# Windowed attention and a squared-ReLU MLP in one kernel: batches three to seven as one run of key tiles, with a refitted DMA model in the planner

## The chip, the cores and the metric

The kernel runs on one core of one Trainium2 chip. The metric is the device time of one execution in microseconds; lower is better. The engines are TensorE (PE; PEld is its weight load), VectorE (DVE), ScalarE (ACT), GpSimd (POOL) and SyncE (SP), each with its own queue of instructions that it works off in order. SP and ACT also issue DMAs.

## What is computed

The inputs q, k and v are float32 of 8 batches x 8 heads x 576 positions x 64. Attention is local: a position sees those at most 32 away. Its result, as 4608 tokens of 512, goes through an MLP.

```python
scores = q @ k.T / sqrt(64)                  # per batch and head
scores = where(abs(i - j) <= 32, scores, -1e9)
x = softmax(scores) @ v                      # -> (4608, 512), token = batch*576 + position
h = maximum(x @ w_in, 0.0)                   # 512 -> 2048
out = (s * h * h + b) @ w_out                # 2048 -> 512
```

## The kernel before

**Attention by units.** Keys are cut in tiles of 64. A unit is two neighbouring key tiles of one batch, stacked on the 128 partitions; a batch has 9 tiles, so five units, the fifth with a single tile (`NTILE = 9`, `NUNIT = 5`, `tiles`, L589). For each key tile, `qk_part` (L592) multiplies the 64 keys with a window of 128 queries, from 32 before the tile to 32 after it, for all 8 heads: 16 small matmuls into the PSUM tensor SC for a full unit. `exp_mask` (L606) takes the exponential on ACT (L620) and multiplies it by a band mask on VectorE (L624), which zeroes what is further than 32 away. `av_part` (L632) then multiplies with V (L650); each 64-query piece sums up to two key tiles, one of them perhaps in the unit before. V has a 65th column of ones, so that the same matmul gives the softmax sum. `finish` (L662) takes the reciprocal (L670), normalizes into XN (L672), and transposes the 128 or 96 finished tokens into XT: on TensorE and ACT for batches 0 to 2 (L679, L684; `XPE = 3`), with DMA transposes issued by SP from batch 3 on (L690). XT is a ring of 2048 token columns. One TensorE task of a unit joins the AV of the unit before and the scores of its own (`pe_part`, L695; `LAG = 1`), and the scores are put between the two halves of the AV.

**Loads.** Batches 0 and 1 come through SP (L493, L478) and are transposed on TensorE (L505). From batch 2 on ACT issues the loads (`LATE = 2`): q and k in three pieces per batch (`piece`, L523: 512 rows of q, 512 of k, the last 64 of both), V in one load per unit (`load_v`, L474, five staging slots VST). Each q/k piece is cast to bf16 in two halves (L543), on the engines that `CASTE` names: both on GpSimd for batch 2, both on VectorE for the batches after. SP then transposes it by DMA (L550), q straight into QT, k into KTR, from where GpSimd copies it in order into KT (L560), four or five copies per batch. QT and KT have two slots, used in turn by the batches. V is cast into VB (L485), two tensors of five slots.

**The MLP.** Tokens are worked in blocks of 96, 128, 288 and then eight of 512. `s1` (L838) computes 16 tiles of h^T (L849), ReLU on ACT (L856) and the square on VectorE (L858); `s2` (L862) multiplies with w_out (L867), L880 adds what s and b give, and SP stores the result (L884).

**Who sets the order.** Nothing here is in order by the program text. `add` (L75) makes a task with its engine, an estimated cost, what it reads and writes, a key and a slack. `plan` (L106) plays the whole kernel through with these costs: it takes, again and again, the task that can start first (ties by key), and so fixes each engine's queue. DMAs are in the play too: a load has a number of rows and a price per row (`dma=("l", 16, 92.0)`), the rings of SP and ACT share the bandwidth (`serve`, L119), a task that reads a loaded buffer is planned to start `slack` ns after the load's planned end at the earliest (`release`, L155), and an issue from ACT waits until its ring has at most `CALM` rows left (`space`, L139). The keys are due times: `due` (L403) asks when the MLP block that holds a unit's first token begins. `emit` (L212) writes the queues with the semaphores that the dependences need: on the chip the order is fixed, and an engine whose next task isn't ready stands still. The loads up to batch 1 have keys below -100 and are chained in a fixed order on SP.

The lines of `plan` that set when the engine is free again after it issues a DMA:

```python
            full = max(st, space(t.stream, self.RING))
            if t.dma[0] == "t":
                free[t.stream] = full + t.cost
            else:
                free[t.stream] = max(st + t.cost, full)
```

Of the kernel before, what the change touches and what calls it, by code (L numbers as in the profile page):

```python
# [10 lines left out]
S = 576  # L11
# [7 lines left out]
NUNIT = (NTILE + 1) // 2  # L19
VW = 66  # L20
# [9 lines left out]
XPE = 3  # L30
PACE = ((-1, -1, -1),) * 3
CASTS = 20.0
LATE = 2
AFTERV = 4
KTV = 0
CASTE = (("pool", "pool"), ("dve", "dve"))
SLACK = (1000.0, 2000.0, 3000.0, 3000.0)
# [23 lines left out]
class _Graph:  # L61
# [6 lines left out]
    RING, CALM, ISSUE, WRITE = 112.0, 40.0, 1400.0, 600.0  # L68
# [37 lines left out]
    def plan(self):  # L106
# [63 lines left out]
        while len(order) < len(self.tasks):  # L170
            best = None
            for s in self.STREAMS:
                for t in open_[s]:
                    at = max(free[s], t.ready)
                    if s == "act" and t.dma is not None:
                        at = max(at, space(s, self.CALM))
                    c = (at, t.key, t.n)
                    if best is None or c < best[0]:
                        best = (c, t)
            st = best[0][0] if best else 1e9  # L180
            done, clock[0] = serve(rings, clock[0], max(st, clock[0]))
            room.clear()
            if done is not None:
                done.fin = clock[0] + self.WRITE
                release(done)
                continue
            assert best is not None, "a cycle"
            t = best[1]
            open_[t.stream].remove(t)
            t.start = st  # L190
            free[t.stream] = t.fin = st + t.cost
            order.append(t)
            for u in t.next:
                u.left -= 1
                if u.left == 0:
                    open_[u.stream].append(u)
            if t.dma is None:
                release(t)
                continue
# [4 lines that stand above are left out]
                free[t.stream] = max(st + t.cost, full)  # L204
            rings[t.stream].append([t, (full if t.dma[0] == "t" else st) + self.ISSUE, float(t.dma[1])])
            room.clear()
        self.order = order
# [96 lines left out]
def bass_sliding_window_symmetric__then__act_starrelu_kernel(  # L304
# [22 lines left out]
    with ExitStack() as es:  # L327
# [24 lines left out]
        VB = [sb((128, NUNIT, H, VW), BF16, "vb") for _ in range(2)]  # L352
        EXS = sb((128, NEX, 2, NPAIR, 128), BF16, "ex")
        EX = [EXS[:, i, :, :, :] for i in range(NEX)]
        MASK = sb((128, 128), BF16, "mask")
# [43 lines left out]
        def unit_rows(m):  # L399
            lo = max(0, 128 * m - WIN)  # L400
            return lo, min(S, 128 * m + 128 - WIN)

        def due(b, m):  # L403
            tok = b * S + unit_rows(m)[0]
            blk = next(x for x in range(NM) if TBLK[x][0] + TBLK[x][1] > tok)
            f = (tok - TBLK[blk][0]) / TBLK[blk][1]
            before = PH[blk] - PH[blk - 1] if blk > 0 else 4.0
            return PH[blk] - 14.0 - (1.0 - f) * before
# [20 lines left out]
        for p0 in (0, 64):  # L429
            band(MASK[p0:p0 + 64, :], ONESW[p0:p0 + 64, :], ("MASK", p0), 0, 64, -96)  # L430
        for i in range(2):
            for c0 in (0, WIN + S):
                zero("dve", QT[i][:, :, c0:c0 + WIN], ("QTZ", i, c0), 150, key=-98 if i == 0 else -20)
            add("dve", lambda e, i=i: e.memset(VB[i].rearrange("p t h c -> p (t h) c")[:, :, D:D + 1], 1.0), 150,
                writes=[("VBO", i)], key=-57 if i == 0 else -20)
# [12 lines left out]
        def load_weights(which, i, x, key, eng):  # L448
# [6 lines left out]
            else:  # L455
# [4 lines left out]
                dma=("l", 16, 92.0) if which == "in" else ("l", 32, 50.0))  # L460
# [5 lines left out]
        def paced(b, u):  # L466

            return land["av", b - 1, u] if u >= 0 else land["av", b - 2, NUNIT + u]

# [4 lines left out]
        def load_v(b, t, key, waits=()):  # L474

            n = min(128, S - 128 * t)
            add(late(b),
                lambda e: e.dma_start(VST[0:n, t, :, :], v[b, :, 128 * t:128 * t + n, :].rearrange("h p d -> p h d")),  # L478
                650.0, writes=[("VST", t)], key=key, dma=("l", n // 2, 23.0), waits=waits)
            land["v", b, t] = g.tasks[-1]  # L480

        def cast_v(b, t, key, eng, slack):
            slot, n = b % 2, min(128, S - 128 * t)
            add(eng, (lambda e: e.copy(VB[slot][0:n, t, :, 0:D], VST[0:n, t, :, :])) if eng == "act" else
                (lambda e: e.tensor_copy(VB[slot][0:n, t, :, 0:D], VST[0:n, t, :, :])),  # L485
                {"act": 617.0, "dve": 420.0, "pool": 750.0}[eng],
                reads=[("VST", t)], writes=[("V", slot, t)], key=key, slack=slack)

        def load_pair(b, name, pr, key, load_key, banks, eng, slack):
# [6 lines left out]
                600.0, writes=[("STG", si)], key=load_key, dma=("l", 8, 112.0))  # L496
# [26 lines left out]
        def piece(b, parts, key, waits):  # L523
# [16 lines left out]
                dma=("l", sum(n for _, _, n, _ in parts) // 8, 68.0))  # L540
# [26 lines left out]
        def later(b, key):  # L567
# [6 lines left out]
            for i, parts in enumerate(((("q", 0, 512, 0),), (("k", 0, 512, 0),), (("q", 512, 64, 0), ("k", 512, 64, 32)))):  # L574
                piece(b, parts, key + 0.01 * i, [paced(b, PACE[min(b, 4) - 2][i])] +
                      ([land["v", b - 1, AFTERV]] if b > (1 if LATE == 2 else 2) and AFTERV >= 0 else []))
# [8 lines left out]
        def buffers(b, u):  # L585
            n = b * NUNIT + u
            return EX[n % NEX], n % NEX, EX[(n - 1) % NEX], (n - 1) % NEX

        def tiles(u):  # L589
            return [j for j in (2 * u, 2 * u + 1) if j < NTILE]  # L590

        def qk_part(b, u, hps=(0, 1)):  # L592
            slot = b % 2
            fns = [lambda e, pr=pr, j=j, hp=hp: e.matmul(  # L594
                SC[64 * (j % 2):64 * (j % 2) + 64, hp, pr * 128:pr * 128 + 128],
                lhsT=KT[slot][64 * hp:64 * hp + 64, pr, 64 * j:64 * j + 64],
                rhs=q_window(b, pr, j)[64 * hp:64 * hp + 64], start=True, stop=True)
                for pr in range(NPAIR) for j in tiles(u) for hp in hps]
            lo, hi = max(0, 128 * u - WIN), min(S, 128 * u + 128 + WIN)
            reads = [("QT", slot, x, pr) for x in pieces(lo, hi, 64) for pr in range(NPAIR)]  # L600
            reads += [("KT", slot, x, pr) for x in tiles(u) for pr in range(NPAIR)]
            if u == 0:
                reads.append(("QTZ", slot, 0))
            if u == NUNIT - 1:
                reads.append(("QTZ", slot, WIN + S))
            return fns, reads, [("SC", hp) for hp in hps], 230.0 if len(hps) == 2 or u == NUNIT - 1 else 440.0  # L606

        def exp_mask(b, u, hps=((0, 1),)):
            key = due(b, u)
            ex, ei, _, _ = buffers(b, u)  # L610
            n = 64 * len(tiles(u))
            for hs in hps:
                dst, src = ex[0:n, hs[0]:hs[-1] + 1, :, :], SC[0:n, hs[0]:hs[-1] + 1, :].rearrange("p i (a c) -> p i a c", a=NPAIR)
                flat = dst.rearrange("p i a c -> p (i a) c")
                if b > 1:
                    flat_src = src.rearrange("p i a c -> p (i a) c").rearrange("p a (i c) -> p a c i", i=4)
                    flat_dst = flat.rearrange("p a (c i) -> p a c i", i=4)
                else:
# [4 lines left out]
                mask = MASK[0:n, :].rearrange("p (one c) -> p one c", one=1).to_broadcast((n, 4 * len(hs), 128))  # L623
                add("dve", lambda e, flat=flat, mask=mask: e.tensor_tensor(flat, flat, mask, ALU.mult),  # L624
                    130 + 0.53 * 512 * len(hs), reads=[("E", ei, hp, pr) for hp in hs for pr in range(NPAIR)] + [("MASK", p0) for p0 in (0, 64)],
# [6 lines left out]
        def av_part(b, u):  # L632


            slot = b % 2
            ex, ei, px, pi = buffers(b, u)
            bank, res = av_banks(b, u)
# [3 lines left out]
            def put(h, x, g):  # L641
# [3 lines left out]
                if not 0 <= j < NTILE:  # L645
                    return []
# [6 lines left out]
                    rhs=VB[slot][64 * g:64 * g + 64, j // 2, h, 0:D + 1], start=first, stop=True,  # L653
# [4 lines left out]
            reads = [("E", x, hp, pr) for x in ({ei, pi} if u > 0 else {ei}) for hp in (0, 1) for pr in range(NPAIR)]  # L658
            reads += [("V", slot, x) for x in ({u, u - 1} if u > 0 else {u})] + [("VBO", slot)]
            return fns, reads, res, 340.0  # L660

        def finish(b, u, key=None):  # L662
            key = due(b, u) if key is None else key
            n = b * NUNIT + u
            bank, avr = av_banks(b, u)
            av = bank.rearrange("p i (a c) -> p (i a) c", a=4)
            r0, r1 = unit_rows(u)
# [9 lines left out]
            if b < XPE:  # L677
# [8 lines left out]
            else:  # L686
                cuts = {x0, x0 + r1 - r0} | {x for x in range(XR, B * S, XR) if x0 < x < x0 + r1 - r0}
                cuts = sorted(cuts | ({x0 + WIN} if u == 0 else set()))
# [42 lines left out]
        def first_exp(dst, src, np_, sc, res, key):  # L731
# [5 lines left out]
                130 + 0.53 * 256 * n, reads=res + [("MASK", p0) for p0 in (0, 64)], writes=res, key=key)  # L737
# [8 lines left out]
        def unit(b, u):  # L746

            ripe = last[0] if len(last) >= LAG else None
            t = pe_part(due(*(ripe or (b, u))), av_part(*ripe) if ripe else None, qk_part(b, u))
# [5 lines left out]
        def close(t=None):  # L755
# [3 lines left out]
            closed[0] = bu[0] * S + unit_rows(bu[1])[1]  # L759
# [3 lines left out]
        def attention():  # L763
# [27 lines left out]
            for t in ORDER0:  # L791
                if t < 8:
                    load_v(0, t, nxt())
# [9 lines left out]
            for t in range(NUNIT):  # L803
                load_v(1, t, nxt())
# [8 lines left out]
            for b in range(2, B):  # L813
                later(b, due(b, 0) - 24.0)
                for t in range(NUNIT):
                    load_v(b, t, due(b, t) - 35.0, waits=[paced(b, PACEV[min(b, 4) - 2][t])] + ([land["kt", 2, 0]] if b == 2 and KTV else []))
                    cast_v(b, t, due(b, t) - 4.0, EV2[t], SLACK[3])
                for u in range(NUNIT):
                    unit(b, u)
                    yield closed[0]  # L820
            while last:
                close()
# [170 lines left out]
```

The softmax here doesn't subtract the row's maximum and nothing guards it: scores larger than these inputs give would overflow.

## Time and profile before

| | |
|---|---|
| median of 6 runs | 326.03 us (323.84 to 328.3) |
| the profiled execution | 327.07 us |
| its span, first to last instruction | 325.3 us |
| TensorE busy | 297.9 us (92%) |
| VectorE busy | 205.4 us (63%) |
| ScalarE busy | 141.0 us (43%) |
| GpSimd busy | 66.8 us (21%) |
| DMA | 56.70 MB, mean 174 GB/s |
| w_in matmuls L849, w_out matmuls L867 | 140.9 us, 139.6 us busy |
| exponentials L620 | 35 of 1023 ns mean |
| mask multiplies L624 | 35 of 742 ns mean |
| q/k casts L543 | 30 of 676 ns mean on VectorE, 6 on GpSimd |
| K copies L560 | 30 of 1072 ns mean on GpSimd |
| DMA transposes into XT, L690 | 32 |

The span is what the trace covers; the execution's own time is 1.8 us longer. A row of waits has the engine and line that waited, what released it, the time in all, how often, and the longest. A row of a timeline has start, duration, engine and line, operation, tiles (out<-in) and how many neighbouring instructions are merged in it; brackets hold the idle time before. "SPq" and "ACTq" are issues of DMAs from these engines' queues: their duration is how long the queue was held.

### The profile page before, as it was taken

The numbers are of one execution on the slowest core, as the hardware profiler recorded it, in microseconds if no ns is written. First come the engines' busy times: TensorE is split into PE (matmuls) and PEld (weight loads), VectorE is DVE, ScalarE is ACT, GpSimd is POOL, SyncE is SP. The second block draws the span as 40 slices with busy tenths as digits, with TensorE's granted clock in tenths as the row PEclk, the third lists the DMA queues.
The fourth block names the chain that finished last, engine by engine and source line by source line (L and its number), as shares of the span: only waits on it lengthen the run. The fifth ranks groups of instructions, "written<-read, shape, count | busy, mean of one in ns | idle before, by whom it ended". The sixth has DMA issues, their size and how long they took to land.

```text
span 325.3 us, 8084 instructions
## 1 busy us (share of the span) xinstructions
PE 297.9 (92%) x3410; PEld 162.6 (50%) x3452; DVE 205.4 (63%) x402; ACT 141.0 (43%) x219; POOL 66.8 (21%) x78
## 2 busy tenths in 40 slices
PE   3687898999998997989999999999999999999995
PEld 2575676755554443444444444444444444444442
DVE  2752588876878894679767868786865443332411
ACT  3645366445523772445225553553454433333200
POOL 3346455464106000420060006000600000000000
PEclk9999999999999999999999999999999999999999
DMA  7999999897896999899948995999612111000021
GB/s 235 280 241 348 360 229 335 279 206 212 202 229 185 268 123 128 177 302 134 249 124 251 166 222 116 195 222 218 154 57 67 50 46 62 34 32 32 34 94 68
DMA packets 104580, 56.70 MB, mean 174 GB/s; under 512 B 77216, under 2 KB 96160, under 8 KB 104544
## 3 DMA queue, kind: packets, MB, share of 16 engines
q1 hardware_dynamic: 62208, 34.94, 44.1%
q10 hardware_dynamic: 42336, 21.24, 31.0%
q8 instruction: 27, 0.44, 0.6%
q14 instruction: 9, 0.07, 0.1%
HBM read 36.70 MB, written 9.44 MB: 142 GB/s over the span
## 4 chain that ended last, share of the span: by engine, by line
PE 73%; DMA 15%; DVE 6%; issue 3%; POOL 1%; ACT 1%; SPq 0%; POOLq 0%
PE o L867 33%; PE w L849 31%; DMA stg<-in_moe_w_in_dram 5%; PE avn L650 4%; DMA stg<-in_moe_w_out_dram 3%; DMA vst<-in_v_dram 3%; DMA xt<-xn 3%; PE sc L594 2%; DVE ex L624 1%; PE o L890 1%; DVE gt L858 1%; DVE xn L672 1%; DVE vb L485 1%; PE sc L505 1%; DMA stg<-in_q_dram 1%
## 5 line engine op out<-in xcount | busy, mean ns | idle before, releaser
L849 PE MATMUL w<-xt,win 128*128 128x512 bf16 (+3 forms) x679 | 140.9, 344 | 6.3 <-issue 2.4
L867 PE MATMUL o<-wout,gt 128*128 128x512 bf16 (+1 forms) x623 | 139.6, 357 | 4.9 <-DVE wout L462 2.4
L856 ACT ACTIVATE r<-w 128x512 bf16<-128x512 f32 (+2 forms) x152 | 86.7, 575 | 115.8 <-PE w L849 99.9
L858 DVE TENSOR_TENSOR gt<-r 128x512 bf16<-128x512 bf16 (+2 forms) x152 | 72.8, 484 | 72.1 <-ACT r L856 71.2
L867 PEld LDWEIGHTS o<-wout,gt 128*128 128x128 bf16 x640 | 60.9, 98 | 64.4 <-DVE wout L462 2.7
L849 PEld LDWEIGHTS w<-xt,win 128*128 128x128 bf16 x704 | 61.9, 101 | 60.0 <-ACT r L856 2.4
L560 POOL COPY kt<-ktr 128x512 bf16<-128x512 bf16 (+1 forms) x30 | 32.2, 1072 | 131.7 <-DMA ktr<-nat 130.2
L620 ACT ACTIVATE ex<-sc 128x1024 bf16<-128x1024 f32 (+1 forms) x35 | 35.8, 1023 | 29.9 <-PE avn L650 24.5
L880 DVE SCALAR_TENSOR_TENSOR outs<-o,sb,cvec 128x512 f32<-128x512 f32 (+1 forms) x40 | 27.6, 691 | 16.6 <-PE o L867 16.4
L624 DVE TENSOR_TENSOR ex<-ex,mask 128x1024 bf16<-128x1024 bf16 (+1 forms) x35 | 26.0, 742 | 4.6 <-ACT ex L620 3.7
L672 DVE TENSOR_TENSOR xn<-avn,rec 128x512 bf16<-128x512 f32 (+1 forms) x34 | 23.4, 687 | 0.8
L650 PE MATMUL avn<-vb,ex 64*64 64x65 bf16 x976 | 22.0, 199 | 2.0 <-ACT xt L684 0.9
L485 DVE CAST vb<-vst 128x512 bf16<-128x512 f32 (+1 forms) x32 | 22.3, 701 | 0.5 <-DMA vst<-in_v_dram 0.4
L650 PEld LDWEIGHTS avn<-vb,ex 64*64 64x64 bf16 x976 | 14.3, 108 | 16.0 <-issue 7.6
L543 DVE CAST nat<-stg 128x1024 bf16<-128x1024 f32 (+1 forms) x30 | 19.7, 676 | 0.0
L594 PE MATMUL sc<-qt,kt 64*64 64x128 bf16 x504 | 14.8, 217 | 0.0
L505 PE MATMUL w<-ident,nat 64*64 64x64 bf16 x144 | 5.6, 240 | 6.4 <-ACT nat L498 4.3
L670 DVE RECIPROCAL rec<-avn 128x8 f32<-128x8 f32 (+1 forms) x34 | 6.8, 201 | 6.9 <-PE avn L650 6.7
L462 POOL CAST win<-stg 128x1024 bf16<-128x1024 f32 x8 | 8.5, 1068 | 10.5 <-DMA stg<-in_moe_w_in_dram 10.5
L594 PEld LDWEIGHTS sc<-qt,kt 64*64 64x64 bf16 x504 | 9.8, 107 | 0.6 <-POOL kt L560 0.4
L462 POOL CAST wout<-stg 128x1024 bf16<-128x1024 f32 x6 | 6.7, 1118 | 10.1 <-DMA stg<-in_moe_w_out_dram 10.1
L505 PEld LDWEIGHTS w<-ident,nat 64*64 64x64 bf16 x144 | 4.7, 150 | 7.2 <-ACT nat L498 4.3
(63 smaller groups left out, 102.3 us busy)
## 6 DMA issues: line engine op xcount, KB each, us to landing
out_dram<-outs SPq DMA_DIRECT2D x32, 256.0 KB, 2.3
vst<-in_v_dram ACTq DMA_DIRECT2D x24, 256.0 KB, 6.0
stg<-in_q_dram ACTq DMA_DIRECT2D x6, 1024.0 KB, 5.6
stg<-in_k_dram ACTq DMA_DIRECT2D x6, 1024.0 KB, 8.8
stg<-in_moe_w_in_dram SPq DMA_DIRECT2D x8, 512.0 KB, 8.3
stg<-in_moe_w_out_dram SPq DMA_DIRECT2D x8, 512.0 KB, 10.4
stg<-in_q_dram SPq DMA_DIRECT2D x8, 288.0 KB, 6.0
stg<-in_k_dram SPq DMA_DIRECT2D x8, 288.0 KB, 6.0
```

What stands on the lines that cost most here:

```text
L485: (lambda e: e.tensor_copy(VB[slot][0:n, t, :, 0:D], VST[0:n, t, :, :])),
L560: add("pool", lambda e, c=c, w=w: e.tensor_copy(KT[slot][:, :, c:c + w].rearrange("p a (s i) -> p a s i", i=4), KTR[slot][:, :, :, c // 4: ...
L594: fns = [lambda e, pr=pr, j=j, hp=hp: e.matmul(SC[64 * (j % 2):64 * (j % 2) + 64, hp, pr * 128:pr * 128 + 128], lhsT=KT[slot][64 * hp:64 * ...
L620: add("act", lambda e, dst=flat_dst, src=flat_src: e.activation(dst, src, AF.Exp, bias=0.0, scale=0.125), 190 + 0.833 * 512 * len(hs), rea ...
L624: add("dve", lambda e, flat=flat, mask=mask: e.tensor_tensor(flat, flat, mask, ALU.mult), 130 + 0.53 * 512 * len(hs), reads=[("E", ei, hp, ...
L650: return [lambda e: e.matmul(av[64 * x:64 * x + 64, h, 0:D + 1], lhsT=buf[64 * g:64 * g + 64, h % 2, h // 2, c:c + 64], rhs=VB[slot][64 * ...
L672: add("dve", lambda e: e.tensor_tensor(XN[xi][0:p1, :].rearrange("p (a c) -> p a c", a=H), av[0:p1, :, 0:D], REC[ri][0:p1, :].rearrange("p ...
L849: add("pe", [lambda e, g=g, kc=kc: e.matmul(wt[:, g, :], lhsT=WIN_BF[:, kc, (f0 + g) * 128:(f0 + g + 1) * 128], rhs=XT[:, kc, t0 % XR:t0 % ...
L856: add("act", lambda e: e.activation(rt, wt, AF.Relu, bias=0.0, scale=1.0), 190 + 0.833 * ng * nt, reads=[("W", wb)], writes=[("R1", rb)], ...
L858: add("dve", lambda e: e.tensor_tensor(GT[gs][:, f0:f0 + ng, g0:g0 + nt], rt, rt, ALU.mult), 130 + 0.53 * ng * nt, reads=[("R1", rb)], wri ...
L867: add("pe", [lambda e, fc=fc: e.matmul(O[:, ob, 0:cn], lhsT=GT[gs][:, fc, g0:g0 + 128], rhs=WOUT_BF[:, fc, c0:c0 + cn], start=(fc == 0), s ...
L880: add("dve", lambda e: e.scalar_tensor_tensor(OUTS[us][:, 0:cn], O[:, ob, 0:cn], SB128[:, 0:1], CVEC[:, c0:c0 + cn], ALU.mult, ALU.add), 2 ...
```

## The change

Batches 0 to 2 stay as they are (`LONG = 3`). The 45 key tiles of batches 3 to 7 become one sequence, cut in pairs: 23 units, numbers 15 to 37. Where a batch ends in the middle of a pair, the unit has the last tile of one batch and the first of the next; two units do (`group_of` tells which units are loaded with which batch). The query windows still come from each batch's own q with its zeroed edges, so what a key tile gives to the windows beyond its batch must not count: three further masks are made on GpSimd at the start, each a copy of the band mask with one or two strips of 32 columns zeroed, and `mask_of` picks one of the four per unit. A straddling unit's V is loaded by two DMAs. VB is one ring of ten slots. The pieces into which a unit's DMA transpose to XT is cut are chosen anew.

In the planner, after the issue of a DMA transpose SP is now held until its ring has at most `PUSH` = 95 rows left. Prices of loads are changed (w_in 92 to 103 per row, w_out 50 to 48.5, V of batches 0 and 1 23 to 21, q/k of batch 1 112 to 98, pieces issued by ACT 68 to 61), slacks are shortened, the key of the q/k casts is 40 after the piece's instead of 20, and from batch 3 on the first half of each piece is cast on GpSimd, the second on VectorE.

```diff
+LONG = 3
+PAIRS = 2
-XPE = 3
+XPE = 15
-CASTS = 20.0
+CASTS = 40.0
-AFTERV = 4
-KTV = 0
-CASTE = (("pool", "pool"), ("dve", "dve"))
-SLACK = (1000.0, 2000.0, 3000.0, 3000.0)
+CASTE = (("pool", "pool"), ("pool", "dve"))
+SLACK = (1000.0, 1000.0, 2000.0, 2000.0)
...
-    RING, CALM, ISSUE, WRITE = 112.0, 40.0, 1400.0, 600.0
+    RING, PUSH, CALM, ISSUE, WRITE = 112.0, 95.0, 40.0, 1400.0, 600.0
...
             room.clear()
+            if t.dma[0] == "t":
+                free[t.stream] = max(free[t.stream], space(t.stream, self.PUSH))
...
-        VB = [sb((128, NUNIT, H, VW), BF16, "vb") for _ in range(2)]
+        VB = sb((128, 2 * NUNIT, H, VW), BF16, "vb")
...
-        MASK = sb((128, 128), BF16, "mask")
+        MASKS = [sb((128, 128), BF16, "mask") for _ in range(4)]
+        MASK = MASKS[0]
...
+        def seq_of(b):
+            return min(b, LONG)
+        def seq_tiles(c):
+            return NTILE * (1 if c < LONG else B - LONG)
+        def seq_units(c):
+            return (seq_tiles(c) + 2) // 2
+        def tile_at(c, t):
+            return c + t // NTILE, t % NTILE
+        def number(c, u):
+            return c * NUNIT + u
+        def group_of(b):
+            if b < LONG:
+                return range(NUNIT)
+            u0 = (NTILE * (b - LONG)) // 2
+            return range(u0, (NTILE * (b + 1 - LONG) + (b == B - 1)) // 2)
...
+        def mask_of(c, u):
+            ends = [tile_at(c, t)[1] for t in tiles(c, u)]
+            if c < LONG or u == 0:
+                ends = []
+            if ends[1:] == [0]:
+                return 1
+            if ends[1:] == [NTILE - 1] and 2 * u + 2 < seq_tiles(c):
+                return 2
+            return 3 if ends[:1] == [0] else 0
+
+        for i, cuts in ((1, ((0, 96), (64, 0))), (2, ((64, 96),)), (3, ((0, 0),))):
+            add("pool", lambda e, i=i: e.tensor_copy(MASKS[i][:, :], MASK[:, :]), 250,
+                reads=[("MASK", 0, 0), ("MASK", 0, 64)], writes=[("MASK", i, 0), ("MASK", i, 64)], key=0.0)
+            for p0, c0 in cuts:
+                add("pool", lambda e, i=i, p0=p0, c0=c0: e.memset(MASKS[i][p0:p0 + 64, c0:c0 + WIN], 0.0), 150,
+                    writes=[("MASK", i, p0)], key=0.0)
...
-                dma=("l", 16, 92.0) if which == "in" else ("l", 32, 50.0))
+                dma=("l", 16, 103.0) if which == "in" else ("l", 32, 48.5))
...
-                600.0, writes=[("STG", si)], key=load_key, dma=("l", 8, 112.0))
+                600.0, writes=[("STG", si)], key=load_key, dma=("l", 8, 112.0 if b == 0 else 98.0))
...
-                dma=("l", sum(n for _, _, n, _ in parts) // 8, 68.0))
+                dma=("l", sum(n for _, _, n, _ in parts) // 8, 68.0 if late(b) == "sp" else 61.0))
...
-            if b < XPE:
+            if n < XPE:
...
-                cuts = sorted(cuts | ({x0 + WIN} if u == 0 else set()))
+                if p0 or x0 + WIN in cuts:
+                    cuts |= {x0 + WIN, x0 + WIN + 32 - p0}
+                cuts = sorted(cuts)
...
-            for b in range(2, B):
-                later(b, due(b, 0) - 24.0)
-                for t in range(NUNIT):
-                    load_v(b, t, due(b, t) - 35.0, waits=[paced(b, PACEV[min(b, 4) - 2][t])] + ([land["kt", 2, 0]] if b == 2 and KTV else []))
-                    cast_v(b, t, due(b, t) - 4.0, EV2[t], SLACK[3])
-                for u in range(NUNIT):
-                    unit(b, u)
+            for b in range(PAIRS, B):
+                c = seq_of(b)
+                later(b, due(c, group_of(b)[0]) - 24.0)
+                for i, u in enumerate(group_of(b)):
+                    load_v(c, u, due(c, u) - 35.0, late(b), [paced(b, PACEV[min(b, 4) - 2][i])])
+                    cast_v(c, u, due(c, u) - 4.0, EV2[i], SLACK[3])
+                for u in group_of(b):
+                    unit(c, u)
                     yield closed[0]
```

## Prediction

> **What bounds the kernel now.** I read the page's busy times and slices first, then the table of stages, TensorE's waits by stage, and the timelines of SP, VectorE and GpSimd around the largest waits.
>
> ```profile
> PE   3687898999998997989999999999999999999995
> DVE  2752588876878894679767868786865443332411
> ```
>
> Two of the page's lines of slices, each slice 8.1 us. TensorE is half idle in the first three slices and then at 9 nearly to the end; VectorE has 8s and a 9 between slices 5 and 15. The table of stages puts numbers on it (busy us and instruction counts):
>
> ```profile
> 66.00:140.00 74.00, 68.52 (x771) 35.89 (x776) 55.77 (x103) 35.87 (x55) 19.98 (x19) 1.00 1.03 197
> 140.00:322.00 182.00, 177.31 (x1589) 85.17 (x1616) 107.28 (x211) 72.13 (x109) 16.41 (x16) 1.00 0.59 127
> ```
>
> The first two times of a row are its length and TensorE's busy time. At 66 us the first 512-token block of L849 starts; from there TensorE misses 5.5 us up to 140 and 4.7 us from 140 to 322. The remainder, 322 to 325.3, is the last output. So TensorE sets the end: a change gains what it takes out of TensorE's own queue, out of these 10 us, or out of the start before 66. Its waits between 66 and 140:
>
> ```profile
> PE w L849 <- DMA xt<-xn: 1.9, 1, 1.9
> PE avn L650 <- ACT xt L684: 0.9, 1, 0.9
> PE w L849 <- issue: 0.8, 5, 0.2
> PE w L849 <- ACT r L856: 0.7, 3, 0.4
> PE o L867 <- issue: 0.6, 4, 0.2
> PE avn L679 <- DVE xn L672: 0.3, 1, 0.3
> ```
>
> The "issue" rows, 0.16 us each, follow an attention burst (AV, scores, AV) when TensorE goes back to the MLP. After 140 the same list has 2.9 us of them, 0.9 us for one mask multiply and 0.3 us for L856. The wait of 1.9 us is at 128.8, and SP's queue before it shows its cause:
>
> ```profile
> 113.56 7.24 SPq L550 DMA_TRANSPOSE qt<-nat  x1
> 120.85 4.56 SPq L690 DMA_TRANSPOSE xt<-xn  x3
> 125.45 5.89 SPq L550 DMA_TRANSPOSE ktr<-nat  x1
> ```
>
> One transpose of q held SP for 7.24 us, and three transposes of finished tokens stood behind it; the MLP waited for one of them. ACT was held 3.94 us by one V load at 121.3 in the same congestion (DMA share 1.03 over the stage), which is the 0.42 us wait on L856 at 125.6.
>
> **What the skill says.** "SBUF — State Buffer", section "Who interferes with whom": VectorE in a two-port mode (copies and casts), or with two SBUF inputs against a GpSimd read, shares a port pair with GpSimd, and the later instruction blocks for the whole of the other. This trace agrees: L485 takes 0.416 us with GpSimd quiet (16 of them) and 1.154 us overlapping one of its instructions (10), L858 0.418 against 0.906 (112 and 20), L624 0.686 against 1.008 (24 and 4), while L672, which reads PSUM, stays at 0.69. "DMA: Bandwidth & Descriptors", section "Issuing engines are not separate DMA queues": SP's and ACT's transfers interleave on the same 16 engines. The trace fits, with both queues held at 121 us. "TensorE: Matmul & The Clock Gate", Part 3: matmuls on different tiles of the array run together. So a unit with one key tile costs what a full one does: its 8 score matmuls at 101.8 take 0.22 us, the full unit's 16 at 97.4 take 0.23.
>
> **The change, part by part.**
>
> *Units.* Batches 3 to 7 have 45 key tiles. Before, that is 5 x 5 = 25 units, each fifth with a single tile; after, 23. The number of 64x64 matmuls hardly falls, since a half-empty unit has half as many, but time does: one burst is 0.25 + 0.23 + 0.21 = 0.69 us on the chain at 97.3, plus 0.16 us of issue. Two bursts fewer are 2 x 0.85 = **1.7 us** of TensorE, on the bounding queue. Elsewhere the two units also take two exponentials (2 x 1.02 us of ScalarE) and on VectorE two mask multiplies (0.78), reciprocals (0.20), normalizations (0.69) and V casts (0.42 to 0.70): 4.2 to 4.7 us. These hide behind TensorE after 140 (VectorE 59% busy there), so I count them at nothing; without that cover they would be worth up to their sum.
>
> *Does a straddling unit arrive later?* It needs the next batch's q, k and v, so the last 32 or 96 tokens of a batch wait for it. But each 512-token MLP block that holds the end of a batch also holds the beginning of the next (batch 3 ends at token 2304, inside block 2048 to 2559; 2880, 3456 and 4032 likewise). No block gets an earlier due time. Cost 0.
>
> *Transposes into XT.* Before 32, as the page counts. After: 23 units, one more for the first unit and two for wraps of the 2048-column ring, 26. At 1.2 us of SP for an unhindered one, SP gets 6 x 1.2 = 7.2 us back. V loads: 23 units, two of them in two halves, 25 issues as before, the second half costing ACT 0.37 us.
>
> *Mask setup.* Three copies and five memsets on GpSimd. Nearest row: affine_select of 64x128, 0.36 us apart. 8 x 0.36 = 2.9 us, from 3.2 to 6.1, in a hole that ends at 5.95 with the first q cast on that engine. 0 to 0.2 us late; if a planner put them behind that cast, still 0, as the next hole is 3.3 us. I take 0.1.
>
> *Half of the q/k casts to GpSimd.* For batches 3 to 7, three pieces each: 15 casts of 0.68 us leave VectorE, 10.1 us, and 15 of 1.13 arrive on GpSimd. That is not 10.1 us won: a GpSimd cast that meets L485, L858 or L624 costs that one 0.3 to 0.7 us. At 0.5 each, 7.5 us come back, so VectorE's net relief is some 2.6 us, between -0.4 (0.7 each) and 10.1 (no collision). On TensorE's path I take 0.3 us of new short waits, from 0 to 1; the one mask wait of 0.88 us at 140 happened during five K copies on GpSimd (134.7 to 140.4), and more GpSimd time makes that likelier. Behind a cast on GpSimd stand the K copies L560, and behind those TensorE's scores.
>
> *Planner costs.* The new rule after a transpose keeps SP occupied until its ring has drained, in place of a fixed cost. The 7.24 us above against a planned 2.0 is what it corrects: output stores and transposes that wait for nothing are no longer placed on an SP that is in fact held, and the more urgent transpose is taken when it comes free. I take the 1.87 and 0.42 us waits as gone: **2.3 us**. Bounds: no gain, if the same congestion meets another wait, to 4.4 us, all five long waits (1.87, 0.94, 0.88, 0.42, 0.31) gone. The order of the loads up to batch 1 is a chain fixed by their keys, so the start is limited by the same transfers: 0, with -2 to +2 for the new order of casts and matmuls among them (TensorE's longest wait there after the first data is 2.40 us for a w_out cast at 31.5).
>
> Sum: -1.7 + 0.1 + 0.3 - 2.3 = -3.6 us on this execution's span, 325.3 to 321.7. That execution took 327.07 us, 1.0 above the median 326.03; the same step from the median gives **322.4 us**.
>
> **The rivals.**
> *Only the units count (324.4).* Waits move and don't shrink: DMA is as busy as before, and the transposes of q and k still have to share SP. For it: the DMA share of 1.03 is not lowered by the change. Against: six transposes fewer. 326.0 - 1.7 + 0.1 = 324.4.
> *Slower: batches begin before their keys have landed (330).* The slacks after a DMA fall from 3000 to 2000 ns for a TensorE part, from 2000 to 1000 for K copies, from 3000 to 2000 for V casts; loads on ACT are costed at 61 per row instead of 68. TensorE runs in planned order: a score burst that comes early holds the whole MLP behind it. Batch 4 is just in time now: its first burst starts at 136.0, its first K copy began at 134.68, and TensorE's weight load waited 0.4 us for it. With four batches from 4 to 7 each early by some 1.5 us: 4 x 1.5 = 6, -1.7 -> 330. It decides from (1.7 + 2.3) / 4 = 1.0 us each, where the gain is gone. Against: batch 5's K copies end at 169.2 and its burst is at 170.0, and SP's new occupancy puts transposes later in the plan, which pushes the other way.
> *Better (319).* All long waits go (4.4), and the start gains some 1 us by better costs of weight loads: 326.0 - 1.7 - 4.4 - 1.0 = 319. Against: three of the five waits hang on VectorE's collisions with GpSimd, which increase.
> *The change doesn't do what it says*, the number of units staying at 25, can't be: 45 tiles in pairs are 23.
>
> **How the numbers follow.** Within 1% of the median is 322.8 to 329.3; that is about what a measurement of this kernel can tell from no change (its six runs span 1.4%). Forecast, chance 0.46, own range 320 to 325: 0.28 of it faster, 0.18 within. Only units 0.15: within. Slower rival 0.19: 0.15 slower, 0.04 within. Better 0.20: faster. So faster 0.48, same 0.37, slower 0.15. The range takes the forecast and the units alone whole, most of the better case down to 318 and the lower half of the slower one up to 329.5.
>
> **What would show it.** 23 exponentials at L620's place for batches 3 to 7 (33 in all, 35 before); 26 transposes xt<-xn; the issue waits of TensorE about 0.3 us fewer; no wait of L849 on xt<-xn near 129; SP's longest transpose below 7 us; L543 split 15 on VectorE and 21 on GpSimd, with VectorE's busy time down by less than 15 us. The forecast is wrong if the stage before 66 moves by over 2 us, or if TensorE's list of waits has scores waiting on kt or qt for over a microsecond per batch.

## The result, and the profile after

The changed kernel takes 323.19 us (median of 19 runs) where the kernel before takes 326.30 beside it: ratio 0.9899, interval 0.9873 to 0.9925. Some executions of either kernel are slower by 1.5% or more than its fastest; they count in the medians, not in the ratios. It was measured twice more as part of the experiments: 0.9943 (0.9920 to 0.9966) and 0.9915 (0.9885 to 0.9946). The mean of the three, 0.9919, is 2.6 us of 326. The profiled execution has a span of 321.6 us, 3.7 less than before.

The lines of slices, of the page of the changed kernel:

```profile
PE   3697799999999998999999999999999999999995
DVE  2775476766885873897497578768645543233311
```

In place of TensorE's 8, 7 and 8 in slices 13, 16 and 18 there is one 8, in slice 16. In the table of stages of the changed kernel (length, TensorE, weight loads, VectorE, ScalarE, GpSimd busy; the last matmul ends at 318.2):

```profile
66.00:140.00 74.00, 70.18 (x805) 36.14 (x816) 54.45 (x100) 36.77 (x58) 29.87 (x26) 1.00 1.01 207
140.00:318.20 178.20, 174.44 (x1567) 83.44 (x1592) 99.87 (x193) 68.79 (x105) 25.10 (x23) 1.00 0.59 124
```

TensorE misses 3.8 us in the first of these stages, 5.5 before, and 3.8 in the second, 4.7 before. GpSimd has 10 us more in the first stage and 9 more in the second. Its waits between 66 and 140:

```profile
PE o L938 <- DVE gt L929: 1.3, 1, 1.3
PE w L920 <- issue: 1.1, 7, 0.2
PE avn L709 <- POOL kt L617: 0.4, 1, 0.4
PE w L920 <- ACT r L927: 0.3, 2, 0.2
PE o L938 <- issue: 0.3, 2, 0.2
```

L938 is the w_out matmul (L867 before), L920 the w_in matmul (L849), L929 the square (L858). The wait of L849 on xt is gone; a wait of 1.3 us on a square, at 122.6, is new. SP's queue there:

```profile
111.88 8.11 SPq L607 DMA_TRANSPOSE qt<-nat  x1
120.04 2.58 SPq L753 DMA_TRANSPOSE xt<-xn  x2
122.71 4.77 SPq L607 DMA_TRANSPOSE ktr<-nat  x1
```

It is the picture of before: one q transpose holds SP 8.11 us, with transposes of finished tokens behind it. The block of tokens from 1536 on, for which L849 waited, begins here; TensorE's rows, before and after:

```profile
130.64 0.59 PE L849 MATMUL w<-xt,win 128*128 128x512 bf16 x2 [1.87 <-DMA xt<-xn]
127.42 1.89 PE L920 MATMUL w<-xt,win 128*128 128x512 bf16 x8
```

TensorE doesn't need these tokens later: it was free for them at 128.77 before and at 127.42 after. The tokens come earlier. The transpose that the block waits for is issued at 121.36 (122.16 before), hardly sooner, and lands at 127.12 (130.55 before), 5.8 us after its issue where it took 8.4. So the wait is gone by 0.3 us. Why this transfer was quicker isn't shown.

The new wait comes from the same crowd through another door. Three lines of timelines, of ACT's queue, VectorE and TensorE:

```profile
120.10 3.11 ACTq L533 DMA_DIRECT2D vst<-in_v_dram  x1
123.14 0.43 DVE L542 CAST vb<-vst 128x512 bf16<-128x512 f32 x1 [2.63 <-DMA vst<-in_v_dram]
123.96 1.04 PE L938 MATMUL o<-wout,gt 128*128 128x512 bf16 x4 [1.31 <-DVE gt L929]
```

A V cast held VectorE 2.63 us for a load that hadn't landed, a square stood behind it, and TensorE waited for that square. ACT, held 3.11 us by the issue of a V load, was late with the next ReLU at the same time.

**Which waits are real.** The page gives 3410 matmuls before and 3413 after. A second profile of each, taken in the experiments, has them all (TensorE's line of the page, before and after):

```profile
PE 302.4 (93%) x3452; PEld 161.9 (50%) x3452; DVE 204.8 (63%) x402; ACT 141.0 (43%) x219; POOL 67.1 (21%) x78
```

```profile
PE 301.8 (94%) x3452; PEld 161.6 (50%) x3452; DVE 193.8 (60%) x379; ACT 138.4 (43%) x217; POOL 86.0 (27%) x100
```

In these two TensorE has no "issue" waits of 0.16 us after 66 at all: they were the places of some 40 matmuls that the first traces had lost. All that is left of TensorE's waits between 66 and 140 in the second profile of before is

```profile
PE w L849 <- DMA xt<-xn: 1.6, 1, 1.6
PE avn L650 <- ACT xt L684: 1.0, 1, 1.0
```

and 0.4 us after 140; in the second profile of the changed kernel there is no wait of TensorE in either stage. So the two long waits of before recur in both of its profiles at the same places, and are absent in all profiles of the changed kernel. TensorE's idle time from the first 512-token block on, gaps of any length added up, is 10.0 us before and 7.4 after in the pair with lost records, 3.2 and 0.3 in the pair without: 2.6 and 2.9 us less.

### The profile page after: what moved, and what is told of

It reads as the page before. It is cut to its first block, busy times and chain, and to the rows that moved or that the text cites. A ratio compares the mean times of both kernels' runs of the same rounds, so it can differ in the third digit from the quotient of the medians.

```text
span 321.6 us, 8099 instructions
## 1 busy us (share of the span) xinstructions
PE 297.1 (92%) x3413; PEld 161.3 (50%) x3452; DVE 195.2 (61%) x379; ACT 138.2 (43%) x217; POOL 86.5 (27%) x100
## 4 chain that ended last, share of the span: by engine, by line
PE 73%; DMA 13%; DVE 4%; issue 3%; POOL 2%; ACT 1%; SPq 1%; ACTq 0%; POOLq 0%
PE o L938 34%; PE w L920 30%; DMA vst<-in_v_dram 5%; PE avn L709 4%; DMA stg<-in_moe_w_out_dram 3%; DMA ktr<-nat 3%; DMA stg<-in_moe_w_in_dram 2%; PE sc L651 2%; PE o L961 1%; DVE ex L683 1%; ACT r L927 1%; DVE gt L929 1%; SPq L505 1%; PE sc L562 1%; DVE xn L733 1%
## 5 line engine op out<-in xcount | busy, mean ns | idle before, releaser
L938 PE MATMUL o<-wout,gt 128*128 128x512 bf16 (+1 forms) x631 | 142.5, 359 | 4.7 <-DVE wout L508 2.4
L920 PE MATMUL w<-xt,win 128*128 128x512 bf16 (+3 forms) x674 | 141.0, 344 | 5.5 <-issue 3.0
L929 DVE TENSOR_TENSOR gt<-r 128x512 bf16<-128x512 bf16 (+2 forms) x152 | 76.8, 510 | 73.4 <-ACT r L927 72.6
L938 PEld LDWEIGHTS o<-wout,gt 128*128 128x128 bf16 x640 | 61.6, 98 | 66.3 <-DVE wout L508 2.7
L920 PEld LDWEIGHTS w<-xt,win 128*128 128x128 bf16 x704 | 61.2, 100 | 58.5 <-ACT r L927 1.6
L679 ACT ACTIVATE ex<-sc 128x1024 bf16<-128x1024 f32 (+1 forms) x33 | 33.8, 1023 | 29.8 <-PE avn L709 27.0
L600 POOL CAST nat<-stg 128x1024 bf16<-128x1024 f32 (+1 forms) x21 | 25.6, 1219 | 52.4 <-DMA stg<-in_q_dram 27.7
L733 DVE TENSOR_TENSOR xn<-avn,rec 128x512 bf16<-128x512 f32 (+1 forms) x32 | 22.0, 689 | 0.9
L709 PE MATMUL avn<-vb,ex 64*64 64x65 bf16 x976 | 20.8, 199 | 1.0 <-POOL kt L617 0.4
L542 DVE CAST vb<-vst 128x512 bf16<-128x512 f32 (+1 forms) x30 | 17.4, 579 | 3.1 <-DMA vst<-in_v_dram 3.1
L651 PE MATMUL sc<-qt,kt 64*64 64x128 bf16 x504 | 13.4, 216 | 0.0
L600 DVE CAST nat<-stg 128x1024 bf16<-128x1024 f32 (+1 forms) x15 | 10.4, 692 | 0.3
L651 PEld LDWEIGHTS sc<-qt,kt 64*64 64x64 bf16 x504 | 8.8, 107 | 0.6 <-issue 0.6
```

The lines of the kernel that those rows point to most:

```text
L600: add(eng, lambda e, x=x: e.tensor_copy(nat[0:top, 1024 * x:1024 * x + 1024].rearrange("p (i h d) -> p h i d", h=H, i=2), stg[0:top, :].re ...
L651: fns = [lambda e, pr=pr, x=x, b=b, j=j, hp=hp: e.matmul(SC[64 * x:64 * x + 64, hp, pr * 128:pr * 128 + 128], lhsT=KT[b % 2][64 * hp:64 * ...
L679: add("act", lambda e, dst=flat_dst, src=flat_src: e.activation(dst, src, AF.Exp, bias=0.0, scale=0.125), 190 + 0.833 * 512 * len(hs), rea ...
L709: return [lambda e: e.matmul(av[64 * x:64 * x + 64, h, 0:D + 1], lhsT=buf[64 * g:64 * g + 64, h % 2, h // 2, c:c + 64], rhs=VB[64 * g:64 * ...
L733: add("dve", lambda e: e.tensor_tensor(XN[xi][0:p1, :].rearrange("p (a c) -> p a c", a=H), av[0:p1, :, 0:D], REC[ri][0:p1, :].rearrange("p ...
L920: add("pe", [lambda e, g=g, kc=kc: e.matmul(wt[:, g, :], lhsT=WIN_BF[:, kc, (f0 + g) * 128:(f0 + g + 1) * 128], rhs=XT[:, kc, t0 % XR:t0 % ...
```

## Experiments

Each ratio is to the kernel before on the same chip. Where a line is given in a diff, the rest is the changed kernel.

**1. The units alone.** The merged sequence, with all the planner's old settings.

```diff
-CASTS = 40.0
-CASTE = (("pool", "pool"), ("pool", "dve"))
-SLACK = (1000.0, 1000.0, 2000.0, 2000.0)
+CASTS = 20.0
+CASTE = (("pool", "pool"), ("dve", "dve"))
+SLACK = (1000.0, 2000.0, 3000.0, 3000.0)
...
-            if t.dma[0] == "t":
-                free[t.stream] = max(free[t.stream], space(t.stream, self.PUSH))
...
```

and the prices 92, 50, 23, 112 and 68 again; the planned cost of issuing a V load from ACT is 650 ns again too, which is 500 in the changed kernel.

> Merged units with all the planner's old settings: old prices, slacks, no PUSH, casts of batches 3 to 7 on VectorE. Queue theory: two bursts less, 326.3 - 1.7 = 324.6 us, ratio 0.995. Planner theory: 1.000. If a straddling unit really delays a batch's end, over 1.000, with TensorE waiting for scores' or AV's operands at the straddling units.

Measured 324.12 us, 0.9953 (0.9922 to 0.9985): 1.5 us less. Its TensorE queue is instruction for instruction that of the kernel before for the first 1676 matmuls, up to 118 us, so little but the units differs until there. TensorE's waits between 66 and 140 are 1.0 us for ACT's copy of batch 2's tokens (as before) and two below 0.7, and after 140 there is none. So no straddling unit waits. The wait for xt near 129 is gone here too, with all the old settings: the transpose lands at 126.98 and the block begins at 127.15. So the 1.5 us can't be put down to the two bursts alone; what a burst is worth is read from experiment 2.

**2. What a unit's TensorE time is worth.** The same queues, with the scores of the 23 merged units issued twice.

```diff
+            fns = fns * 2 if c >= LONG else fns
             reads = []
```

> The changed kernel with the score matmuls of its 23 merged units issued twice (the second time over the same result); planned costs and so all queues stay as they are. It measures what a unit's TensorE time is worth. Queue theory: 23 x 0.23 = 5.2 us longer than the changed kernel, 328.3 us where before is 326.3, ratio 1.006. If TensorE had hidden room beside its waits (the units are worth nothing), the same as the changed kernel, 0.990. Half of it, 0.998, would mean that a saved burst of 0.85 us is worth some 0.4.

Measured 328.41 us, 1.0085 (1.0055 to 1.0115). Against the changed kernel's 0.9919 that is 0.0166 x 326.2 = 5.4 us for 360 matmuls more (4.6 to 6.1 with the highest and the lowest of its three ratios), 0.235 us per unit, where the chain shows 0.23 for one score burst. Time added to a unit on TensorE counts in full, with the queues held fixed: the queue theory holds. That time taken away counts the same is argued from it.

**3. The settings alone.** Five units per batch as before, everything else new.

```diff
-LONG = 3
+LONG = 8
...
-            if seq_tiles(LONG) % 2 == 0:
+            if LONG < B and seq_tiles(LONG) % 2 == 0:
```

> The planner's new settings alone (LONG = 8): every batch keeps its five units, prices, slacks, PUSH and the split casts are the new ones. Queue theory (TensorE is full, two bursts of 0.85 us are worth 1.7 us wherever they are saved): about 1.7 us of the change's 3.3 us are missing, so 324.8 us where before is 326.3, ratio 0.995, with 35 exponentials at the unit line and DMA transposes into XT back at 32. Planner theory (the saved units lie beside other waits and give nothing; the new settings give it all): the same as the whole change, ratio 0.990. If new settings are worth nothing by themselves: 1.000.

Measured 325.38 us, 0.9988 (0.9959 to 1.0016): 0.4 us less at best estimate, 1.3 at most. That is less than either theory gave, and what settings that are worth nothing by themselves would give. And yet TensorE stands still for only 0.65 us from the first 512-token block on in its profile, with all records; the kernel before stands 3.2. In this profile what was won late was lost earlier: the first 512-token block begins at 70.2 us, where it began at 66.0 before and 66.4 after. The wait for xt is gone here too, by less than 0.1 us: the transpose lands at 129.98, and the block begins at 130.04.

**4. The casts back on VectorE.**

```diff
-CASTE = (("pool", "pool"), ("pool", "dve"))
+CASTE = (("pool", "pool"), ("dve", "dve"))
```

> The changed kernel with the first halves of the q/k casts back on VectorE from batch 3 on. My theory: VectorE's net relief by the move is small (GpSimd's casts lengthen the squares and V casts that they meet), so the time is that of the changed kernel within 1 us, ratio 0.987 to 0.993; VectorE's busy time 5 us or so higher than 195 and the mean of the squares of 128x512 back from 0.53 towards 0.49 us. Rival: the relief of VectorE by 10 us is what gives the gain: the time goes back by 1.5 us or more, ratio 0.995.

Measured 323.49 us, 0.9932 (0.9906 to 0.9959), inside the span of the changed kernel's three values. VectorE is busy 198.3 us here and 195.2, 193.8 and 198.2 in the three profiles of the changed kernel: the move of some 10 us of casts relieves it by 2.6 at the mean, by 0.1 to 4.5 against the single profiles; 5 us were expected. The squares show where nearly half of the rest goes; VectorE's row of the groups by shape, of the changed kernel and of this one:

```profile
L929 DVE TENSOR_TENSOR gt<-r 128x512 bf16<-128x512 bf16 x132 | 69.4, 530 | 67.3 <-ACT r L927 66.7
```

```profile
L929 DVE TENSOR_TENSOR gt<-r 128x512 bf16<-128x512 bf16 x132 | 65.9, 504 | 67.5 <-ACT r L927 66.8
```

In the changed kernel 36 of these squares overlap a GpSimd instruction and take 0.824 us, the other 96 take 0.420; before it was 20 and 112, and in this run it is again.

**5. The old prices in the start.** A late start in experiment 3 and in two other profiles led to a new theory: the refit's order of the start gives back what the late stage wins. So the loads up to batch 1 were priced as before.

```diff
-                dma=("l", 16, 103.0) if which == "in" else ("l", 32, 48.5))
+                dma=("l", 16, 92.0) if which == "in" else ("l", 32, 50.0))
...
-21.0 if c < 2 else 23.0
+23.0
...
-112.0 if b == 0 else 98.0
+112.0
```

> The changed kernel with the old prices for the loads up to batch 1 (w_in 92, w_out 50, V 23, q/k of batch 1 112 per row): its TensorE queue is that of the kernel before up to the last units of batch 1 (some 60 us), and everything after has the new settings. Start theory: the refit's new order in the start costs what the late stage wins, as the first 512-token block began at 70.2, 69.8 and 72.7 us in three of four profiles with the new start, against 66.0 and 66.0 in the two with the old one. Then the block begins at 66 to 67 here and the time is 2 us below the changed kernel's, 321.0 us, ratio 0.984. Rival, chance: the late starts are executions with half-clock phases and late w_out loads that any order can meet; then the ratio is that of the changed kernel, 0.990, within 0.003.

Measured 326.15 us, 0.9972 (0.9939 to 1.0005): not faster, rather slower than the changed kernel beside it (0.9943). The first block began at 67.7. The theory isn't borne out. It isn't refuted either: the start came out differently from the old one too (TensorE's queue leaves that of the kernel before at matmul 716, 47 us, not at some 60 as expected), and this run is one more draw of the plan, which experiment 10 prices at 2.4 us.

**6. Second profiles.** The changed kernel measured again, and one run of the kernel before.

> The changed kernel once more, for a second profile and a comparison on the same chip as the run with old prices in the start. Ratio 0.990 as before. Start theory: the first 512-token block begins at 68 us or later in this profile. Chance: anything between 66 and 72.

> The kernel before, for a second profile of its start. Start theory: the first 512-token block begins at 66 to 67 us again. Chance: later than 68 us is as likely as in the new start.

The changed kernel 0.9943, first block at 68.5; the kernel before 327.46 us in its one run, first block at 67.7. The start varies for both: over the 14 profiles of this study the first block begins at 66.0 to 72.7, and in 10 of them TensorE runs at half clock for 3.4 us or more at some time before 66, the second profile of before among them with 13.6 us. In the four profiles with the old prices in the start it begins at 66.0 to 67.7, in the ten with the new ones at 66.4 to 72.7, 1.5 us later at the mean. So a cost of the new start is neither shown nor excluded.

**7. The sequence from batch 2 on.**

```diff
-LONG = 3
+LONG = 2
```

> The sequence from batch 2 on (LONG = 2): 54 tiles are 27 units and one closing AV, so batches 2 to 7 cost 27 score and mask steps where the changed kernel has 28. Queue theory: one score burst of 0.23 us and one switch less, about 0.4 us, 322.8 us, ratio 0.9885, which these runs can't tell from 0.990. Rival: batch 2's end now waits for batch 3's keys, and the time is over 0.993.

Measured 325.38 us, 0.9963 (0.9932 to 0.9993), beside the changed kernel's 0.9943. The two intervals overlap; the expected 0.4 us can't be seen, and the rival can't be told from the draw of the plan, that is from what another order of the same work gives by chance (experiment 10).

**8. The second column sum later.** In four of the six profiles with the new start up to here TensorE waited 1.1 to 2.3 us at L961 for the last w_out cast, in the changed kernel's first profile not.

```diff
-                1760, reads=["ONESW"] + [("Wout", i, x) for i in range(4)], writes=[("O", ob)], key=P2[0])
+                1760, reads=["ONESW"] + [("Wout", i, x) for i in range(4)], writes=[("O", ob)], key=P2[0],
+                waits=[land["av", 1, 3]] if x else [])
```

> The changed kernel with one more order in the start: the column sum of the second half of w_out (L961, the second of the two) is planned behind the AV of batch 1's fourth unit. In four of five profiles with the new start TensorE waits there 1.1 to 2.3 us for the last w_out cast, in the old start not. If that wait is part of what the refit costs at the start: no such wait in the profile, and 1 to 1.5 us less than the changed kernel on the same chip. If TensorE only waits a little later for something else there (a q/k of batch 1 or the tokens of the first 512 block): the same ratio as the changed kernel within 0.003.

Measured 321.79 us, 0.9906 (0.9867 to 0.9945), beside 0.9915 for the changed kernel on this chip: the same. The wait is 1.0 us, ending at 63.5, where the changed kernel's profile of the same chip has 1.7, ending at 60.0. The cast that it waits for had itself stood 1.76 us for its load.

**9. Without PUSH.**

```diff
-            if t.dma[0] == "t":
-                free[t.stream] = max(free[t.stream], space(t.stream, self.PUSH))
```

> The changed kernel without PUSH: SP is free again after a transpose at its fixed cost in the plan. My prediction's step: PUSH removes the wait for xt near 129 us, so it is back, with SP held again by a q transpose ahead, and the time 1.5 to 2 us above the changed kernel's on this chip. Rival: TensorE's queue is that of the changed kernel up to beyond that place (its first 2097 matmuls are in the same order), so the wait isn't back and the time is the changed kernel's within 0.003: PUSH wasn't what removed it.

Measured 323.28 us, 0.9948 (0.9921 to 0.9976), beside 0.9915; the intervals overlap. The wait for xt near 129 is not back: TensorE goes from w_out to w_in without a pause, though SP is held just as long. SP's and TensorE's timelines of this kernel:

```profile
112.63 7.49 SPq L605 DMA_TRANSPOSE qt<-nat  x1
120.16 3.86 SPq L751 DMA_TRANSPOSE xt<-xn  x3
124.11 3.83 SPq L605 DMA_TRANSPOSE ktr<-nat  x1
```

```profile
126.69 1.03 PE L936 MATMUL o<-wout,gt 128*128 128x512 bf16 x3
127.56 1.89 PE L918 MATMUL w<-xt,win 128*128 128x512 bf16 x8
129.28 1.03 PE L936 MATMUL o<-wout,gt 128*128 128x512 bf16 x4
```

The transpose lands at 127.25, the block begins at 127.56. PUSH isn't what removed that wait.

**10. Another plan of the same work.** `MARGIN` is the time, in ns, that the planner adds before TensorE may use another engine's result.

```diff
-    MARGIN = 250.0
+    MARGIN = 260.0
```

> The changed kernel with the planner's MARGIN at 260 ns instead of 250: no work is added or removed, the plan falls out differently from early on. It shows how much the draw of a plan is worth by itself. If single settings can be told apart at this level: the changed kernel's ratio within 0.002. If plans differ by chance as much as the settings seemed to: 0.003 or more away from it, to either side.

Measured 325.77 us, 0.9988 (0.9955 to 1.0022), beside 0.9915 for the changed kernel: 2.4 us slower, with the same work and settings. Its waits of TensorE between 66 and 140:

```profile
PE w L920 <- ACT r L927: 1.5, 3, 1.1
PE avn L709 <- POOL kt L617: 1.2, 1, 1.2
PE avn L709 <- ACT xt L745: 1.0, 1, 1.0
PE w L920 <- issue: 0.7, 4, 0.2
PE o L938 <- issue: 0.6, 4, 0.2
PE o L938 <- DVE gt L929: 0.3, 1, 0.3
```

The wait of 1.0 us for ACT's copy, which both profiles of before have and the changed kernel hasn't, is here again. A plan that differs by 10 ns in one estimate is worth nearly as much as the whole change. That bounds the reading of experiments 1, 3 to 5 and 7 to 9 too: each of them is also another plan.

**11. The changed kernel a third time**, as the measure for 8, 9 and 10.

> The changed kernel a third time, as the measure for the other three on this chip: ratio between the two values so far, 0.990 and 0.994.

Measured 322.14 us, 0.9915. Its profile has the wait on the square near 122.7 again, with 0.9 us.

## Why the prediction was right, point by point

**The bound and the units: right.** TensorE sets the end, and its time in a unit counts one to one (experiment 2: 5.4 us for 5.2 expected). Two units fewer were put at 1.7 us; the plan with them alone gave 1.5 (0.5 to 2.5), in which the vanished wait for xt and the draw of that plan are mixed. Inside the 0.85 us per unit, 0.69 is the burst; the 0.16 us of issue was no wait but a lost record, so the term should have been 2 x 0.69 = 1.4.

**Straddling units without delay, mask setup, XT transposes: right.** The only long wait at a straddling unit is the first one's, 0.4 us for batch 4's keys; before, batch 4's own first unit stood at that place, with a weight load 0.4 us late. The transposes are 26 (the list of DMA issues), the exponentials of the unit line 33. At the start TensorE waits 0.8, 1.5 and 1.3 us for GpSimd's second q cast in the changed kernel's three profiles, 1.1 and 2.0 in the two of before: the mask setup costs nothing that can be seen. The start as a whole was put at 0, within 2 us either way; the first block began at 66.0 and 67.7 before and at 66.4, 68.5 and 66.4 after, which fits.

**The casts: right in kind.** VectorE's relief was put at 2.6 us net, out of 10.1; experiment 4 has 2.6 at the mean. That the two agree to a tenth is luck, as single profiles give 0.1 to 4.5; that it is far below 10 is shown, and the squares that collide with GpSimd are nearly half of the reason. That this costs TensorE 0.3 us is neither shown nor excluded.

**The planner's settings, -2.3 us: wrong in its cause, and too large.** TensorE's late waits did fall by 2.6 to 2.9 us, about the size predicted. But the step said why: that PUSH keeps urgent transposes from standing behind a q transpose. SP's longest q transpose is 8.11 us, not below 7; the transposes behind it wait as before; without PUSH the xt wait doesn't return; it is gone with the old settings as well (experiment 1); the settings alone are worth 0.4 us; and the same settings with another draw of the plan have as much idle time late as the kernel before (9.8 us, 10.0 before, 7.4 after, all with lost records). If the units are worth the 1.4 to 1.5 us above, what lies between that and the whole, 2.6 - 1.5 = 1.1 us, goes with this one plan, and no setting that was tried alone can be named as its owner. The step went wrong where it took one wait in one trace for something that the rule controls. The sum came within 1 us of what was measured although the cause of its largest term was wrong: that part is luck.

**"Only the units count" (324.4 us)** isn't beaten. The gain forecast was 3.6 us, this rival's 1.6; the three measures of the changed kernel give 1.9 to 3.3 and 2.6 at the mean, midway. **The better case (319 us)** didn't come, though in the second profile TensorE stands only 0.3 us from the first 512-token block on.

**The slower rival** exists on a small scale: the first burst with batch 4's keys waits for them 0.4 and 0.6 us in two of the changed kernel's profiles, up to 0.9 in experiments 1 to 9 and 1.2 in experiment 10, but at one batch, not at four, and in the changed kernel below the point of 1.0 us each from which it would have decided.

**Open.** Why the unprofiled gain (2.6 us by the mean of three) is smaller than that of the spans (325.3 and 325.7 before; 321.6, 321.0 and 321.6 after) wasn't settled; the scatter of the start is larger than the difference. Nor was it settled why the settings alone, with 2.6 us less idle time late in their profile, give 0.4 us.

## What to carry to other kernels

When a queue is full, price a saving by its busy time on that engine's chain and test it by doubling the work with the queues held fixed: that gave 5.4 us for 5.2 expected, while undoing single settings of a planner gave differences that a 10 ns change of an estimate gives too. A wait that is gone in the trace says little of its cause where the data come 0.1 to 0.3 us before they are needed. Before crediting a setting, measure how far a meaningless change of the same planner moves the time. And a small regular "issue" gap after every burst is to be checked against the count of records before it is priced.

## What the runs showed of the hardware

The port that VectorE shares with GpSimd ("SBUF — State Buffer", section "Who interferes with whom", of the Trainium skill) shows in this case's traces: a square of 0.42 us becomes 0.78 to 0.91 at the mean of a profile of the two kernels when a GpSimd cast or copy overlaps it, a V cast of 0.42 becomes 0.86 to 1.15. Of some 10 us of casts moved to GpSimd VectorE was relieved of 2.6 at the mean, 0.1 to 4.5 by single profiles. A DMA transpose of finished tokens landed 5.8 us after its issue in one kernel and 8.4 in the other, at the same place in the work. TensorE's granted clock fell to half for stretches of 3.4 us or multiples (10.2, 6.8) in the loading phase, before 66 us, in 10 of 14 profiles, and between there and the end of the MLP in none. In the 3.4 us before each of these 13 falls TensorE was busy for 53% of the time at most, and in 12 of them no single gap within some microseconds reached 3.4 us: the longest was 1.0 us near the fall at 56.4 in experiment 9's profile and 1.2 near the one at 57.2 in experiment 4's.
